# Seven PSUM banks as slices of one tensor, and reductions and exponentials of two banks at once

## The chip, the cores and the metric

The kernel runs on one core of a Trainium2 chip. The core has TensorE (PE in the profile, its weight loads PEld), VectorE (DVE), ScalarE (ACT), GpSimd (POOL) and SyncE (SP), which issues the transfers. TensorE writes its results to PSUM, eight banks of 512 fp32 columns on 128 partitions. The metric is the device time of one execution in microseconds, lower is better.

## The reference

One transformer block on x of 2048 tokens by 512, all in fp32: a layer norm with scale and shift from a condition c, attention with 32 heads of 16, and a spatial-shift MLP.

```python
qkv = (x @ wqkv).reshape(B, S, 3, H, Dh).transpose(2, 0, 3, 1, 4)
q, k, v = qkv[0], qkv[1], qkv[2]
scores = jnp.einsum("bhqd,bhkd->bhqk", q, k) * (Dh ** -0.5)
p = _softmax(scores, axis=-1)
o = jnp.einsum("bhqk,bhkd->bhqd", p, v)
...
x = x + ga * _A_ref(h, A_wqkv, A_wo)
h = _layernorm(x, axis=-1) * (1 + cb) + sb
x = x + gb * _B_ref(h, B_w1, B_w2, B_w3, B_w4)
```

The change touches the scores and the softmax, and none of the rest.

## The kernel before, in words

The kernel has three stages. The first normalizes x and makes q, k and v of the first heads. The second, the attention, goes over 64 units (4 chunks of 512 queries by 16 pairs of heads), with 16 steps of 128 keys in each unit, 1,024 steps in all. The rest of the projections is mixed into it, and the beginning of the MLP into its end. The third stage is the MLP.

A step s has two halves, one for each head of the pair (j = 0, 1). A half step makes one score tile (`sc`: 128 keys by 512 queries, `score_part`) and, `LEAD` = 24 steps ahead, one maxima tile (`mb`: 128 queries by 512 keys, `max_part`). The matmuls of these two use different halves of TensorE's rows, so they are written next to each other (`row_pair`). DVE takes the maximum of each row of `mb` into `mx` (L992); after 32 such tiles `max_fin` turns the maxima of a unit into two extra rows of q, by 8 small transfers. ACT takes the exponential of `sc` into P (`pt`, L1008). P is stored as 32-bit integers whose upper 16 bits are read as one fp16 part, the lower as another; `p_low` makes the lower part on POOL (L1061) or, where POOL is behind, on ACT (L156). `pv_part` then multiplies both parts by v, four matmuls of 32 columns side by side (L1083, L1086), into one more bank, `pv`.

The order of the instructions is written out by a planner, the class `Sched`, while the program is built: it has a clock for each engine and costs for each instruction, and the main loop goes over blocks of `GRP` = 3 half steps. In a block come the matmuls of three score and three maxima tiles, their evictions, and then three `pv` parts of a block two earlier. What is left of PE's time is filled with projection work by `sch.fill`. The class `Slots` holds when each of the `NSM` = 7 shared banks comes free, by the planner's clock. Before, each bank is a tensor of its own, made anew for each tile under one of seven tags, and takes the slot that is free first. Projection tiles and the small `ot` tile (`o_fin`, a transposition of the sum) take their banks from the same seven (`dbank`).

The semaphores that each instruction waits for do not stand in the code. They are put in when the program is built, from the tensors that the instructions read and write.

```python
    def bank(nm):
        x = sm.take()
        return x, ap_.tile([P, CH], F32, name=nm, tag=f"s{x}", bufs=1)
```

Of the kernel before, what the change touches and what calls it, by code (L numbers as in the profile page):

```python
# [20 lines left out]
S, D, H, DH, F = 2048, 512, 32, 16, 1792  # L21
P = 128
KT = D // P
NKT = S // P
CH = 512
NC = S // CH
# [11 lines left out]
LEAD = 24  # L38
# [3 lines left out]
PX = 270.0  # L42
XX = 170.0
XP = {"A": 280.0, "D": 200.0, "G": 200.0}
# [4 lines left out]
CROW, CCOL, CIN, CMID, COUT = 232.0, 240.0, 105.0, 95.0, 67.0  # L49
CFILL = 200.0  # L50
NSM = 7
# [3 lines left out]
LATE = 1e9  # L55
# [41 lines left out]
XCOPY = 0  # L97
NQ = 7
NPT = 6
NV = 3  # L100
DBW, DLAT = 360.0, 2200.0
NST = 4
# [9 lines left out]
class Sched:  # L112
# [29 lines left out]
    def chain(self, *ops, prio=1, ready=None, bank=None):  # L142

        if ready is None:
            ready = self.T["P"] + PX
        n = 0
        while n < len(self.chains) and self.chains[n][2] <= prio:
            n += 1
        bank = bank is not None and id(bank.tensor)
# [100 lines left out]
    def share(self, slots, most):  # L250

        self.avail, self.back, self.owner = [], [], {}
        self.slots, self.most = slots, most

    def take(self, tile):
# [7 lines left out]
        self.owner[id(b.tensor)] = i  # L263
        self.open = id(b.tensor)
        return b

    def free(self, b):

        i = self.owner.pop(id(b.tensor), None)
# [35 lines left out]
class Slots:  # L305
# [7 lines left out]

    def late(self):
        return sum(t == LATE for t in self.t)


def cA(n=CH):
# [12 lines left out]
def kernel(ctx, tc, A_x, A_wqkv, A_wo, B_w1, B_w2, B_w3, B_w4, c, w_mod, out):  # L331
    nc = tc.nc
    te, act, dve, pool, dma = nc.tensor, nc.scalar, nc.vector, nc.gpsimd, nc.sync
# [56 lines left out]
    for j in range(2):  # L390
        x = [ident[:, 64 * j + VD * a:64 * j + VD * a + DH + 1] for a in range(3)]
# [116 lines left out]
    kst, qtl = [], []  # L508
# [226 lines left out]
    for i in range(NV):  # L735
        t = qp.tile([P, H // 4, 192], BF16, name=f"vt{i}")
# [218 lines left out]

    unit_tiles(at, 1, pool, pool)
    qst, vst, mxs = {}, {}, {}
    pv, pt = {}, {}

    def load_unit(u):  # L960
        ci, pr = units[u]
# [11 lines left out]
    sm = Slots(NSM)  # L973
    e_exp, e_hi, e_low, v_free, acs = {}, {}, {}, [0.0], []

    def bank(nm):
        x = sm.take()
        return x, ap_.tile([P, CH], F32, name=nm, tag=f"s{x}", bufs=1)

    def max_part(m, j):  # L980

        u, i = divmod(m, 16)
        c, g = divmod(i, 4)
        if u not in mxs:
            mxs[u] = at.tile([P, 2, 4, NC], F32, name="mx", tag="mx", bufs=2)
        x, b = bank("mb")
        ready, sm.t[x] = sm.t[x], LATE
        r = slice(64 * j, 64 * j + 62)
        lhs = qst[u][r, (g // 2) * 256:(g // 2 + 1) * 256].rearrange("p (n l) -> p l n", l=2)[:, g % 2]

        def after(e):
            end = sch.crit("D", 605, e + PX, lambda: dve.reduce_max(mxs[u][:, j, g, c:c + 1], b, axis=AX.X))  # L992
            sm.t[x] = end + XP["D"]
            if (c, g, j) == (NC - 1, 3, 0):
                max_fin(u)
        return ready, lambda: te.matmul(b, lhs, kst[u % 3][r, c * CH:(c + 1) * CH], start=True, stop=True), after  # L996

    def score_part(s, j):

        u, kt = divmod(s, NKT)  # L1000
        if j == 0:
            pt[s] = at.tile([P, 2, CH], I32, name="pt", tag="pt", bufs=NPT)
        x, b = bank("sc")
        ready, sm.t[x] = sm.t[x], LATE
        r = slice(64 * j, 64 * j + 64)

        def after(e):
            ea = sch.crit("A", 480, e + PX, lambda: act.activation(pt[s][:, j], b, AF.Exp))  # L1008
            sm.t[x] = ea + XP["A"]
            if j:  # L1010
                e_exp[s] = e_hi[s] = ea
        return ready, lambda: te.matmul(b, kst[u % 3][r, kt * P:(kt + 1) * P], qst[u][r], start=True, stop=True), after  # L1012

    def row_pair(s, j):

        parts = []
        if 0 <= s < NS:
            parts.append((j, score_part(s, j)))
        if s + LEAD < NS:
            parts.append((1 - j, max_part(s + LEAD, 1 - j)))  # L1020
        parts = [x for _, x in sorted(parts, key=lambda x: x[0])]

        def mms():
            for _, mm, _ in parts:
                mm()
        e = sch.put("P", CROW, max(x[0] for x in parts), mms)
        return [partial(x[2], e) for x in parts]

    def max_fin(u):
        mf = at.tile([P, 8], F32, name="mf", tag="mf", bufs=2)  # L1030
        nm = at.tile([P, 2, 8], F32R, name="nm", tag="nm", bufs=2)
        mx = mxs.pop(u)

        def shift_rows():
            for j in range(2):
                for i in range(2):
                    r = 64 * j + 62 + i
                    for h in range(2):
                        sch.dma(dma.dma_start,
                                qst[u][r:r + 1, h * 256:(h + 1) * 256].bitcast(F32).rearrange("o (p l) -> o p l", l=2),  # L1040
                                nm[:, i, 4 * j + 2 * h:4 * j + 2 * h + 2].bitcast(F32))
        sch.chain(("D", 85, lambda: dve.reduce_max(mf.rearrange("p (j g) -> p j g", j=2), mx, axis=AX.X)),
                  ("A", 100, lambda: act.activation(mf, mf, AF.Copy, scale=-1.0, bias=PEXP)),
                  ("A", 100, lambda: act.activation(nm[:, 0], mf, AF.Copy)),
                  ("G", 250, lambda: pool.tensor_tensor(nm[:, 1], mf, nm[:, 0], op=OP.subtract)),
                  (None, 0, shift_rows), mark(("shift", u)), prio=0, ready=sch.T["D"])

    def p_low(s):

        p = pt[s].rearrange("p j n -> p (j n)")  # L1050
        o, i = p.bitcast(F16)[:, 0::2], p.bitcast(U16)[:, 0::2]
        ready = e_exp.pop(s) + XX
        g, a = [max(sch.T[e], ready) for e in "GA"]
        if g > a + LACT:

            for h in range(NLOW):
                n = 2 * CH // NLOW
                c = slice(h * n, (h + 1) * n)
                e_low[s] = XP["A"] + sch.crit("A", CLOW, ready, partial(act.activation, o[:, c], i[:, c], AF.Copy, scale=0.5))
        else:  # L1060
            e_low[s] = XP["G"] + sch.crit("G", 1345, ready, lambda: pool.tensor_scalar(  # L1061
                o, i, 0.5, 1.0, op0=OP.mult, op1=OP.mult))
# [5 lines left out]
    def pv_part(s, lo):  # L1068


        u, kt = divmod(s, NKT)
        if kt == 0 and not lo:
            pv[u] = ap_.tile([P, CH], F32, name="pv", tag="v", bufs=1)
        v, acc = vst[u], pv[u]

        def mms():
            for j in range(2):
                for i in range(2):
                    r = 64 * j + 32 * i
                    if lo:  # L1080
                        c = 128 + 32 * j + (0 if i else 8)
                        n = min(32, 192 - c)
                        te.matmul(acc[r:r + n, :], v[:, kt + i, c:c + n].bitcast(F16), pt[s + i].bitcast(F16)[:, j, 0::2],  # L1083
                                  start=False, stop=kt == NKT - 2, skip_group_check=True)
                    else:
                        te.matmul(acc[r:r + 32, :], v[:, kt, r:r + 32], pt[s].bitcast(F16)[:, j, 1::2],  # L1086
                                  start=kt == 0, stop=False, skip_group_check=True)
        e = sch.put("P", CCOL, 0.0, mms)
        if lo:
            for i in range(2):  # L1090
                pt.pop(s + i)
                e_low.pop(s + i)
            if kt == NKT - 2:
                acs.append((u, e + COUT))
# [507 lines left out]
    for k, blk in enumerate(blocks + [[]] * (LAG + CPER)):  # L1602
# [21 lines left out]
        banks = sorted(sm.t)  # L1624
        n = 0
        for s, i in row:
            n += (s >= 0) + (s + LEAD < NS)

            start = max(start, banks[n - 1 + 2 * (s < 0)] - t)
            t += CROW  # L1630
        t += CMID
        for s, i in col:
            start = max(start, pv_ready(s, i) - t)
# [2 lines left out]
        sch.flush(need)  # L1636
        sch.T["P"] = max(sch.T["P"], start) + CIN
        low = sorted(e_exp)
        for s, i in row:
# [91 lines left out]
```

## Time and profile before

| | |
|---|---|
| median of 3 runs | 2018.74 us (2018.37 to 2018.93) |
| profiled execution, span from first to last instruction | 2019.7 us |
| stage 1, up to the first maxima matmul | 96.6 us |
| attention, up to the last `pv` matmul | 1436.7 us |
| stage 3 | 486.4 us |
| mean granted TensorE clock | 0.992 of full speed |

The profiled execution is shown by its span, 0.05% over the median; the two are taken as one. In the page's rows an instruction is named by engine, line, operation and the tiles that it writes and reads (`mx<-mb`), with its count, the busy time in us and the mean of one in ns. A row of waits names the engine that waited and who ended the wait. PEclk is the clock that TensorE was granted, as a share of full speed.

### The profile page before, as it was taken

Reading aid. Unit: us, or ns where it says so; the run is one execution under the profiler, and the core shown is the slowest. Engines: PE = TensorE matmul, PEld = TensorE weight load, DVE = VectorE, ACT = ScalarE, POOL = GpSimd, SP = SyncE. Lnnn points to the kernel's source line nnn. Section 1 sums busy time; section 2 is a strip of 40 time slices with the busy share of each in tenths; the row PEclk is TensorE's granted clock in tenths of the full one; section 3 lists DMA queues with packets and bytes.
Section 4 is the critical chain, followed back from the end, with each engine's and each line's share of the span. In section 5 each row is a group of like instructions: output and inputs, shape, how many; then the busy total and the mean of one; then the engine's idle time right before and its main releaser. Section 6 shows DMA issues by size and latency. Waiting matters only on the chain.

```text
span 2019.7 us, 41655 instructions
## 1 busy us (share of the span) xinstructions
PE 1934.4 (96%) x14456; PEld 1162.1 (58%) x14456; DVE 1656.3 (82%) x2979; ACT 1510.2 (75%) x3085; POOL 1571.9 (78%) x1488
## 2 busy tenths in 40 slices
PE   7999999999999999999999999999998999999999
PEld 5755545454444444444444444444455878898998
DVE  6398888879999999999999999999975886556443
ACT  6438987768999999999999999999985544344443
POOL 6349988879999999999999999999996554435222
PEclk9989999999999999999999999999999999999999
DMA  8777675445343434444443435354414676553541
GB/s 295 233 204 192 151 187 155 135 130 124 86 92 87 91 88 83 96 82 97 81 98 75 104 72 107 72 136 126 99 46 158 230 261 265 226 200 116 201 153 68
DMA packets 185508, 278.01 MB, mean 138 GB/s; under 512 B 117104, under 2 KB 127856, under 8 KB 169008
## 3 DMA queue, kind: packets, MB, share of 16 engines
q1 hardware_dynamic: 181792, 267.20, 49.1%
q10 hardware_dynamic: 2304, 4.20, 0.6%
q0 software_dynamic: 1200, 3.93, 0.5%
q8 instruction: 115, 1.88, 0.4%
q14 instruction: 97, 0.79, 0.1%
HBM read 211.81 MB, written 62.91 MB: 136 GB/s over the span
## 4 chain that ended last, share of the span: by engine, by line
PE 61%; DVE 16%; ACT 9%; issue 6%; POOL 4%; DMA 3%; SPq 0%; ACTq 0%; POOLq 0%; DVEq 0%
PE mb L996 13%; DVE mx L992 12%; PE pv L1086 9%; PE sc L1012 8%; ACT pt L1008 7%; PE w L363 5%; PE w L359 5%; PE w L361 5%; PE pv L1083 4%; PE ot L1113 3%; POOL pt L1061 2%; PE xT L1247 1%; POOL trs L1356 1%; PE v L359 1%; DMA wr<-Ws 1%
## 5 line engine op out<-in xcount | busy, mean ns | idle before, releaser
L1061 POOL TENSOR_SCALAR pt<-pt 128x1024 f16<-128x1024 uint16 x953 | 1248.3, 1367 | 79.9 <-ACT pt L1008 76.7
L992 DVE TENSOR_REDUCE mx<-mb 128x1 f32<-128x512 f32 x2048 | 1250.0, 681 | 72.7 <-PE mb L996 63.5
L1008 ACT ACTIVATE pt<-sc 128x512 int32<-128x512 f32 x2048 | 1060.9, 614 | 123.5 <-PE mb L996 97.1
L996 PE MATMUL mb<-kst,qtl 62*128 62x512 f32 x2048 | 781.1, 461 | 20.5 <-ACT pt L1008 10.0
L1012 PE MATMUL sc<-qtl,kst 64*128 64x512 f32 x2048 | 739.3, 449 | 4.6 <-DVE mx L992 1.8
L996 PEld LDWEIGHTS mb<-kst,qtl 62*128 62x128 f32 x2048 | 358.9, 193 | 233.7 <-ACT pt L1008 160.4
L1012 PEld LDWEIGHTS sc<-qtl,kst 64*128 64x128 f32 x2048 | 336.6, 185 | 185.4 <-DVE mx L992 118.7
L1086 PE MATMUL pv<-pt,vst 128*32 128x512 f16 x4096 | 384.8, 397 | 20.6 <-ACT ac L1103 20.6
L1460 POOL TENSOR_TENSOR g<-sq,g 128x256 fp32r<-128x256 f32 (+1 forms) x124 | 96.8, 785 | 188.9 <-ACT g L1459 176.6
L1083 PE MATMUL pv<-pt,vst 128*32 128x512 f16 (+1 forms) x2048 | 220.8, 389 | 2.5 <-POOL pt L1061 2.4
L1086 PEld LDWEIGHTS <-vst 128*32 128x32 bf16 x4096 | 91.8, 93 | 227.2 <-issue 208.8
L361 PE MATMUL w<-A,wr 128*128 128x256 f32 (+1 forms) x520 | 153.4, 295 | 0.3 <-DVE A L349 0.3
L359 PE MATMUL w<-A,wr 128*128 128x256 f32 (+1 forms) x520 | 153.2, 295 | 0.3 <-ACT A L353 0.3
L363 PE MATMUL w<-A,wr 128*128 128x256 f32 (+1 forms) x520 | 153.1, 294 | 0.0
L1456 ACT ACTIVATE sq<-w 128x256 f32<-128x256 f32 (+1 forms) x130 | 52.1, 401 | 127.0 <-PE w L363 117.5
L363 PE MATMUL w<-wr,g 128*128 128x512 f32 x270 | 106.5, 394 | 3.1 <-POOL g L1460 3.1
L359 PE MATMUL w<-wr,g 128*128 128x512 f32 x270 | 106.9, 396 | 1.8 <-DMA wr<-Ws 1.8
L361 PE MATMUL w<-wr,g 128*128 128x512 f32 x270 | 106.1, 393 | 0.0
L1438 DVE SCALAR_TENSOR_TENSOR sq<-sq,w 128x256 f32<-128x256 f32 (+1 forms) x130 | 58.1, 449 | 56.5 <-ACT sq L1458 56.3
L359 PEld LDWEIGHTS w<-A,wr 128*128 128x128 f32 x520 | 98.7, 190 | 1.7 <-ACT A L353 0.5
L361 PEld LDWEIGHTS w<-A,wr 128*128 128x128 f32 x520 | 98.7, 190 | 1.6 <-DVE A L349 0.5
L363 PEld LDWEIGHTS w<-A,wr 128*128 128x128 f32 x520 | 98.6, 190 | 0.5 <-issue 0.5
(156 smaller groups left out, 2131.6 us busy)
## 6 DMA issues: line engine op xcount, KB each, us to landing
wr<-Ws SPq DMA_DIRECT2D x66, 1024.0 KB, 5.2
vst<-Vs SPq DMA_DIRECT2D x64, 768.0 KB, 5.7
kst<-Ks SPq DMA_DIRECT2D x126, 384.0 KB, 6.1
Ws<-wr SPq DMA_DIRECT2D x14, 1024.0 KB, 5.0
qtl<-Qs SPq DMA_DIRECT2D x128, 96.0 KB, 4.3
Vs<-vt SPq DMA_DIRECT2D x32, 384.0 KB, 4.2
Ks<-qk SPq DMA_DIRECT2D x16, 512.0 KB, 3.8
Qs<-qk SPq DMA_DIRECT2D x16, 512.0 KB, 3.0
```

Source lines behind the costliest of these rows:

```text
L359: te.matmul(o, lh, rh, start=first, stop=False)
L361: te.matmul(o, lh, rl, start=False, stop=False)
L363: te.matmul(o, ll, rh, start=False, stop=last)
L992: end = sch.crit("D", 605, e + PX, lambda: dve.reduce_max(mxs[u][:, j, g, c:c + 1], b, axis=AX.X))
L996: return ready, lambda: te.matmul(b, lhs, kst[u % 3][r, c * CH:(c + 1) * CH], start=True, stop=True), after
L1008: ea = sch.crit("A", 480, e + PX, lambda: act.activation(pt[s][:, j], b, AF.Exp))
L1012: return ready, lambda: te.matmul(b, kst[u % 3][r, kt * P:(kt + 1) * P], qst[u][r], start=True, stop=True), after
L1061: e_low[s] = XP["G"] + sch.crit("G", 1345, ready, lambda: pool.tensor_scalar(o, i, 0.5, 1.0, op0=OP.mult, op1=OP.mult))
L1083: te.matmul(acc[r:r + n, :], v[:, kt + i, c:c + n].bitcast(F16), pt[s + i].bitcast(F16)[:, j, 0::2], start=False, stop=kt == NKT - 2, skip ...
L1086: te.matmul(acc[r:r + 32, :], v[:, kt, r:r + 32], pt[s].bitcast(F16)[:, j, 1::2], start=kt == 0, stop=False, skip_group_check=True)
L1113: te.matmul(b[:, t * n:(t + 1) * n], ac[:, t * P:(t + 1) * P], smat.rearrange("p j d -> p (j d)"), start=True, stop=True)
L1460: ("G", cG(n), lambda: pool.tensor_tensor(lo, sq, hi, op=OP.subtract)), (None, 0, end), bank=b)
```

## The change

The seven banks become the slices `psb[:, i]` of one tensor, and the six buffers of P the slices of one tensor `pts`. Where two tiles of one kind lie in neighbouring banks, DVE reduces both with one instruction of 1,024 columns (`max_out`), and ACT takes the exponential of both with one (`score_out`). In a block of three half steps the first tile of each kind stays single and the other two are joined. `choose` asks `Slots.place` for banks for these groups, and falls back to single tiles if the joined ones would start over 150 ns later by the planner's clock. The maxima `mx` are stored in the order in which the tiles come, and `max_fin` reads them in the permuted order.

```diff
+    psb = ap_.tile([P, NSM, CH], F32, name="psb")
+    pts = at.tile([P, NPT, 2, CH], I32, name="pts")
...
-        return sch.take(lambda i: psd["d"].tile([P, CH], F32, name=n, tag=f"s{i}" if psd["s"] else f"d{i}", bufs=1))
+        return sch.take(lambda i: psb[:, i] if psd["s"] else psd["d"].tile([P, CH], F32, name=n, tag=f"d{i}", bufs=1))
...
-        def after(e):
-            end = sch.crit("D", 605, e + PX, lambda: dve.reduce_max(mxs[u][:, j, g, c:c + 1], b, axis=AX.X))
-            sm.t[x] = end + XP["D"]
+    def max_out(x, ts, e):
+        n = len(ts)
+        u, i = divmod(ts[0][0], 16)
+        o = 2 * i + 1 - ts[0][1]
+        b = psb[:, x:x + n]
+        end = sch.crit("D", 72 + 533 * n, e + PX, lambda: dve.reduce_max(mxs[u][:, o:o + n], b, axis=AX.X))
+        sm.t[x:x + n] = [end + XP["D"]] * n
...
-        def after(e):
-            ea = sch.crit("A", 480, e + PX, lambda: act.activation(pt[s][:, j], b, AF.Exp))
-            sm.t[x] = ea + XP["A"]
+    def score_out(x, ts, e):
+        n = len(ts)
+        s, j = ts[0]
+        o = 2 * (s % NPT) + j
+        p = pts.rearrange("p a j n -> p (a j) n")[:, o:o + n]
+        ea = sch.crit("A", 53 + 427 * n, e + PX, lambda: act.activation(p, psb[:, x:x + n], AF.Exp))
+        sm.t[x:x + n] = [ea + XP["A"]] * n
...
+                n = 2 if two and on and (len(tiles) - i) % 2 == 0 and not cut(tiles[i + 1][1]) else 1
+                out.append((tiles[i:i + n], fn, fin))
...
-        sch.chain(("D", 85, lambda: dve.reduce_max(mf.rearrange("p (j g) -> p j g", j=2), mx, axis=AX.X)),
+        sch.chain(("D", 85, lambda: dve.reduce_max(mf.rearrange("p (j g) -> p j g", j=2),
+                                                   mx.rearrange("p (c g j) -> p j g c", g=4, j=2), axis=AX.X)),
...
-        for s, i in row:
-            for fn in row_pair(s, i):
-                fn()
+        if row:
+            row_pairs(row, *choose(row)[1:])
```

In the built program DVE's 2,048 reductions become 738 single and 655 joined ones, ACT's 2,048 exponentials 696 single and 676 joined; POOL makes 1,020 lower parts of P in the attention stage in place of 952. The matmuls and transfers keep their number. The order of instructions shows what each one waits for, in square brackets: the semaphore of an engine (`PE_49`, `Activation_49` for ACT, `DVE_49`, `Pool_49` for POOL), which counts the instructions that this engine has finished.

DVE before, in the middle of the attention, at the end of a unit (`rc` belongs to the `ot` tile of a unit, `mf` closes the maxima of another):

```order
L992 TENSOR_REDUCE mx<-mb 128x1 [waits PE_49] x30
L1128 RECIPROCAL rc<-sm 128x8 [waits Activation_49,Pool_49]
L992 TENSOR_REDUCE mx<-mb 128x1 [waits PE_49] x2
L992 TENSOR_REDUCE mx<-mb 128x1 [waits DVE_49,PE_49]
L1042 TENSOR_REDUCE mf<-mx 128x8 [waits DVE_49,Pool_49]
```

DVE now, at the end of a unit in the middle of the attention:

```order
L1032 TENSOR_REDUCE mx<-psb 128x1 [waits PE_49]
L1194 RECIPROCAL rc<-sm 128x8 [waits Activation_49,Pool_49]
L1032 TENSOR_REDUCE mx<-psb 128x2 [waits PE_49,Activation_49]
L1108 TENSOR_REDUCE mf<-mx 128x8 [waits DVE_49]
L1032 TENSOR_REDUCE mx<-psb 128x1 [waits Activation_49]
L1032 TENSOR_REDUCE mx<-psb 128x2 [waits Activation_49]
```

Before, a reduction waits for PE's matmul; now most of them, single (128x1) or joined (128x2), wait for ACT as well or for ACT alone.

ACT before, behind the small instructions that close the maxima of a unit:

```order
L1043 ACTIVATE mf<-mf 128x8 [waits DVE_49]
L1044 ACTIVATE nm<-mf 128x8 [waits DMAHW4_49,DMAHW3_49,DMAHW5_49,DMAHW2_49,DMAHW6_49,DMAHW1_49,DMAHW7_49,DMAHW0_49,Activation_49]
L1008 ACTIVATE pt<-sc 128x512 [waits PE_49]
L1008 ACTIVATE pt<-sc 128x512 [waits PE_49,Pool_49]
L1008 ACTIVATE pt<-sc 128x512 [waits PE_49]
```

ACT now, at the same place:

```order
L1110 ACTIVATE mf<-mf 128x8 [waits DVE_49]
L1111 ACTIVATE nm<-mf 128x8 [waits DMAHW4_49,DMAHW3_49,DMAHW5_49,DMAHW2_49,DMAHW6_49,DMAHW1_49,DMAHW7_49,DMAHW0_49,Activation_49]
L1043 ACTIVATE pts<-psb 128x512 [waits PE_49,Pool_49]
L1043 ACTIVATE pts<-psb 128x1024 [waits DVE_49,PE_49,Pool_49]
L1043 ACTIVATE pts<-psb 128x512 [waits DVE_49]
L1043 ACTIVATE pts<-psb 128x1024 [waits DVE_49,Pool_49]
```

Three of these four exponentials wait for a DVE reduction; before, none did.

PE now, the matmuls of one block in the middle of the attention, between two runs of `pv`:

```order
L1150 MATMUL pv<-pts,vst 32x512
L1024 MATMUL psb<-qtl_145,kst_147 128x512 [waits Activation_49]
L1018 MATMUL psb<-kst_967,qtl_965 128x512
L1018 MATMUL psb<-kst_967,qtl_965 128x512 [waits DVE_49]
L1024 MATMUL psb<-qtl_145,kst_147 128x512 x2
L1018 MATMUL psb<-kst_967,qtl_965 128x512
```

and before, of one block there:

```order
L1086 MATMUL pv<-pt,vst 32x512
L1012 MATMUL sc<-qtl_1103,kst_1105 128x512 [waits DVE_49]
L996 MATMUL mb<-kst_967,qtl_965 128x512 [waits Activation_49] x2
L1012 MATMUL sc<-qtl_1103,kst_1105 128x512 [waits DVE_49] x2
L996 MATMUL mb<-kst_967,qtl_965 128x512 [waits Activation_49]
```

Before, each matmul waits for the engine that read its own bank last; now the block has two waits, one ahead of the first half step and one ahead of the other two, on the reader that ran last.

More of the change, by code (lines that the diff above doesn't have):

```diff
@@ L99 @@
 NPT = 6
+DMX, DSC = 1, 1
+DTOL = 150.0
 NV = 3
@@ L148, in chain @@
             n += 1
-        bank = bank is not None and id(bank.tensor)
+        bank = bank is not None and self.key(bank)
         if bank == self.open:
@@ L974, with max_tile @@
     e_exp, e_hi, e_low, v_free, acs = {}, {}, {}, [0.0], []
[L976 to L980, printed above, removed]
+    def max_tile(m, j, b):
         u, i = divmod(m, 16)
@@ L996, in max_part, with score_tile @@
[L996 to L998 removed]
+        te.matmul(b, lhs, kst[u % 3][r, c * CH:(c + 1) * CH], start=True, stop=True)
+    def score_tile(s, j, b):
         u, kt = divmod(s, NKT)
[L1001 to L1004, printed above, removed]
         r = slice(64 * j, 64 * j + 64)
[L1007 to L1009 removed]
+        te.matmul(b, kst[u % 3][r, kt * P:(kt + 1) * P], qst[u][r], start=True, stop=True)
```

112 lines of the change are left out of this document (79 added, 33 removed).

## The prediction

> **What bounds the kernel now.** I read the page's first two lines, then the windows by stage, the groups by line, the chain of waits, and last the order of instructions of both programs with what each waits for.
>
> ```profile
> span 2019.7 us, 41655 instructions
> PE 1934.4 (96%) x14456; PEld 1162.1 (58%) x14456; DVE 1656.3 (82%) x2979; ACT 1510.2 (75%) x3085; POOL 1571.9 (78%) x1488
> ```
>
> The windows cut the span at the first maxima matmul and behind the last `pv` matmul. The columns are the window, its length, busy time and count of each engine, the granted TensorE clock, the DMA share and GB/s:
>
> ```profile
> 0.00:96.60 96.60, 83.53 (x420) 62.77 (x420) 47.06 (x109) 54.21 (x106) 45.72 (x66) 0.98 0.82 265
> 96.60:1533.30 1436.70, 1390.13 (x11313) 687.08 (x11314) 1312.05 (x2273) 1243.27 (x2489) 1324.01 (x1135) 0.99 0.48 111
> 1533.30:2019.70 486.40, 460.79 (x2724) 412.29 (x2722) 297.18 (x597) 212.75 (x492) 202.18 (x287) 0.99 0.52 191
> ```
>
> The attention stage is the middle row, 1436.7 us, and there four engines are each 87 to 97% busy side by side. The change touches only this stage; the 96.6 + 486.4 = 583 us around it stay. The work of the stage by groups (mean ns of one behind the bar, then idle time ahead of it and its releaser):
>
> ```profile
> L992 DVE TENSOR_REDUCE mx<-mb 128x1 f32<-128x512 f32 x2048 | 1250.0, 681 | 72.7 <-PE mb L996 63.5 <-PE sc L1012 5.4
> L1061 POOL TENSOR_SCALAR pt<-pt 128x1024 f16<-128x1024 uint16 x953 | 1248.3, 1367 | 79.9 <-ACT pt L1008 76.7
> L1008 ACT ACTIVATE pt<-sc 128x512 int32<-128x512 f32 x2048 | 1060.9, 614 | 123.5 <-PE mb L996 97.1 <-PE sc L1012 15.3 <-POOL pt L1061 1.2
> ```
>
> DVE and ACT wait for PE (63.5 and 97.1 us in all), hardly for anything else. PE's weight loads wait for a bank that one of them read last:
>
> ```profile
> PEld mb L996 <- ACT pt L1008: 160.4, 464, 0.9
> PEld sc L1012 <- DVE mx L992: 118.7, 303, 2.2
> ```
>
> 2048 score tiles in blocks of three are 683 blocks, so a block takes about 1436.7/683 = 2.1 us, and 1.8 us where no projection work is mixed in: the timeline shows 17 reductions in 10.25 us, 0.603 us each back to back, and three of them are 1.81 us.
>
> ```profile
> 902.21 10.25 DVE L992 TENSOR_REDUCE mx<-mb 128x1 f32<-128x512 f32 x17 [0.42 <-PE mb L996]
> 902.24 3.05 ACT L1008 ACTIVATE pt<-sc 128x512 int32<-128x512 f32 x6 [0.41 <-PE mb L996]
> ```
>
> These two rows also show what matters most here: DVE and ACT read PSUM at the same time, one bank each, for the whole stage, while PE fills others.
>
> **The change, part by part.** Two joined instructions replace two pairs of single ones per block: that saves DVE and ACT each one fixed cost. Against this stands what the order above shows: once all seven banks are one tensor, every DVE reduction that follows an exponential waits for it, every exponential that follows a reduction waits for that, and PE's matmuls wait for whichever came last. Followed through the built program by the counts that its waits name, every one of the 7,897 reads and writes of `psb` stands behind all earlier ones of the other engines, whatever the bank; of the reads and writes of single banks before, almost none did. So the stage becomes one chain, and its time is the sum of the links, not the largest engine.
>
> A block now is: matmuls of the first half step; exponential of 512 and reduction of 512 (in either order, one behind the other); matmuls of the other two half steps; exponential of 1,024 and reduction of 1,024, one behind the other. Two half steps need two pairs of matmuls. The links at full clock and at half clock (the granted clock was 0.50 in 136.25 to 143.07, the windows below):
>
> ```profile
> 901.65 0.49 PE L1012 MATMUL sc<-qtl,kst 64*128 64x512 f32 x1
> 901.65 0.72 PE L996 MATMUL mb<-kst,qtl 62*128 62x512 f32 x2
> 136.57 0.79 PE L1012 MATMUL sc<-qtl,kst 64*128 64x512 f32 x1 [1.84 <-DVE mx L992]
> 137.40 0.60 ACT L1008 ACTIVATE pt<-sc 128x512 int32<-128x512 f32 x1 [1.98 <-PE mb L996]
> 137.77 1.22 PE L1012 MATMUL sc<-qtl,kst 64*128 64x512 f32 x2
> ```
>
> One half step takes 0.50 us at full clock and 0.79 at half, two take 0.74 and 1.22; ACT starts 0.04 after the matmul's end (136.57 + 0.79 = 137.36, 137.40), and alone it takes 0.60. From ACT's end to DVE's start it is 0.03 (1545.05 to 1545.08):
>
> ```profile
> 1544.63 0.42 ACT L1458 ACTIVATE sq<-sq 128x256 f32<-128x256 f32 x1 [0.56 <-DVE sq L1457]
> 1545.08 0.42 DVE L1438 SCALAR_TENSOR_TENSOR sq<-sq,w 128x256 f32<-128x256 f32 x1 [0.48 <-ACT sq L1458]
> ```
>
> From ACT's or DVE's end to the matmul I take 0.05. No instruction of 1,024 PSUM columns runs before; the slopes of two widths give it:
>
> ```profile
> L1457 DVE SCALAR_TENSOR_TENSOR sq<-sq,w 128x256 f32<-128x256 f32 x102 | 42.7, 419 | 32.0 <-ACT sq L1456 27.6
> L1457 DVE SCALAR_TENSOR_TENSOR sq<-sq,w 128x384 f32<-128x384 f32 x28 | 15.3, 551 | 10.7 <-ACT sq L1456 10.7
> L1456 ACT ACTIVATE sq<-w 128x256 f32<-128x256 f32 x102 | 38.6, 378 | 119.8 <-PE w L363 113.2 <-DMA x<-in_A_x_dram 2.6 <-POOL g L1460 0.8
> L1456 ACT ACTIVATE sq<-w 128x384 f32<-128x384 f32 x28 | 13.5, 486 | 7.2 <-PE w L363 4.3 <-POOL g L1460 2.8
> ```
>
> DVE 1.03 ns per column, so 0.68 + 512 x 1.03 = 1.21 us; ACT 0.84, so 0.60 + 0.43 = 1.03. The upper ends are twice the single one, 1.36 and 1.20 (+0.32 per block, +215 us); a lower end under the slope has nothing for it.
>
> Per block at half clock: 0.84 + 0.04 + 0.60 + 0.03 + 0.68, then 1.27 + 0.04 + 1.03 + 0.03 + 1.21 = 5.77 us. At full clock 0.55 and 0.79 stand for 0.84 and 1.27: 5.00 us. 667 blocks have both kinds of tile; the first 16 have maxima alone and the last 16 scores alone (4.08 and 3.81 us at half clock). Half clock: 667 x 5.77 + 16 x 7.89 = 3975 us. Full clock: 667 x 5.00 + 16 x 6.36 = 3437 us.
>
> Other work in `psb` joins the chain: 312 matmuls of 512 and 215 of 256 columns (0.23 and 0.12 us at full clock), 64 times `ot` with its copy, and the evictions of the projections:
>
> ```profile
> 1819.21 0.23 PE w L359
> 1799.96 0.12 PE w L359
> 914.67 1.08 PE L1113 MATMUL ot<-smat,ac 128*128 128x34 f32 x8
> L1120 ACT ACTIVATE sm<-ot 128x136 f32<-128x136 f32 x63 | 18.0, 286 | 20.5 <-PE ot L1113 20.4
> L353 ACT ACTIVATE qk<-q 128x512 fp32r<-128x512 f32 x14 | 8.5, 609 | 2.9 <-PE q L363 2.8
> ```
>
> 72 + 26 + 69 us of PE, and about 85 of ACT and DVE (18 for `sm`, 28 splits at 0.61 with as many subtractions, and 17 `v` tiles): 250 us, at half clock some 380.
>
> What I cost at nothing: `pv`, 12 matmuls a block in three groups of four. At full clock they take 0.86 us (900.86 to 901.72), at half clock some 1.5, by the third row:
>
> ```profile
> 900.86 0.41 PE L1086 MATMUL pv<-pt,vst 128*32 128x512 f16 x4
> 901.32 0.40 PE L1086 MATMUL pv<-pt,vst 128*32 128x512 f16 x4
> 140.28 0.62 PE L1086 MATMUL pv<-pt,vst 128*32 128x512 f16 x4
> ```
>
> They run under the long exponential and reduction (2.3 us). The 1,020 low halves of P, now nearly all on POOL, take 1.37 us each, 1.5 per block, 2.1 of 5.8 us; the ring of P has six slots as before, so its waits reach as far back. The permuted `mf` reduction runs 64 times at some 0.2 us. If `pv` came late, the next block's matmuls would stand behind it on PE.
>
> **The clock.** PE is now idle for most of a block, and the trace shows what short idleness does. Windows of 3.41 us, in pairs or threes that follow each other:
>
> ```profile
> 102.12:105.53 3.41, 2.42 (x6) 0.94 (x6) 3.41 (x7) 1.61 (x5) 0.00 (x0) 1.00 1.11 260
> 105.53:108.94 3.41, 3.41 (x10) 2.28 (x9) 3.41 (x7) 0.29 (x1) 2.94 (x3) 0.50 0.99 157
> 132.83:136.25 3.42, 1.91 (x7) 0.90 (x7) 3.35 (x5) 1.54 (x3) 1.67 (x2) 1.00 1.06 346
> 136.25:139.66 3.41, 2.69 (x10) 1.74 (x10) 3.41 (x7) 1.63 (x4) 2.74 (x3) 0.50 1.09 221
> 139.66:143.07 3.41, 3.41 (x22) 1.42 (x23) 3.41 (x7) 2.93 (x7) 3.41 (x3) 0.50 0.99 203
> 480.99:484.40 3.41, 2.25 (x24) 1.13 (x26) 3.41 (x7) 3.41 (x7) 2.85 (x3) 1.00 1.00 194
> 484.40:487.82 3.42, 3.42 (x34) 2.17 (x27) 2.22 (x4) 2.92 (x7) 3.15 (x3) 1.00 0.48 173
> ```
>
> After 1.91 and after 2.42 us busy of 3.41 (with six or seven matmuls) the clock was 0.50; after 2.25 (24 matmuls) it stayed. At 0.50, 2.69 us busy did not bring it back; fully busy windows came ahead of its return. The changed block at full clock has 0.50 + 0.74 + 0.86 (`pv`) = 2.1 us busy of 5.0, or 1.4 per 3.41: under every one of these, so the clock falls. At half clock it is 0.79 + 1.22 + 1.5 = 3.5 of 5.77, or 2.1 per 3.41, under the 2.69 that did not suffice: it stays down. Only the bursts of projection work in the first fifth of the stage should lift it now and then; I take 85 us off for them. The Trainium skill, "TensorE: Matmul & The Clock Gate", Part 1, has the clock halve after at least one idle window of about 3.4 us and return after a busy one. Taken literally, as no idle time over 3.4 us, it would leave this kernel at full clock, since no link pair here is that long; the row at 132.83, with 1.91 us busy, does not agree with that reading.
>
> Sum at half clock: 583 + 3975 + 380 - 85 = 4853, and some 15 us for copies of `ac` and the like: **4870 us**. Its span and the runs agree (2019.7 against a median of 2018.7), so nothing is added.
>
> **The rivals.** (1) The chain is as told, but the clock stays up, because the gate counts idle stretches and not shares: 583 + 3437 + 250 + 15 = 4285 us. For it: the longest idle stretch of PE in a block is under 2.4 us. Against: the row at 132.83.
> (2) The two readers run beside each other and only PE takes turns with them; then a block is the longer of each two, 0.84 + 0.04 + 0.68 + 1.27 + 0.04 + 1.21 = 4.08 us, and the time 683 x 4.08 + 300 + 583 = 3670 us. It decides if a reader's wait names an access at least a phase back; the order has it at the one just before.
> (3) Faster: the waits are met before they are reached, and the change does what it says. DVE would spend 0.60 + 1.14 = 1.74 instead of 1.81 us per block, at best 0.07 x 683 = 48 us less, 1971 us; POOL, at 1324 of 1437 us, would let some 30 through: 1985 us. It decides if ACT's exponential always ends before DVE's turn comes, which needs idle time that engines over 87% busy do not have. The Trainium skill, "PSUM — Partial Sum Buffer", Specifications, says that ScalarE and VectorE can read PSUM in parallel at full rate if they do not meet in one bank; the rows at 902.21 and 902.24 agree. By that the order between banks is not needed, but the program waits for it all the same.
>
> **How the numbers follow.** The chain at half clock for most of the stage 0.66, at full clock 0.21, (2) 0.09, (3) 0.03, no visible change 0.01 (0.2% is about what the measurement can tell). The range reaches from just under (1) to the likeliest with most of the upper ends of the joined instructions, 4870 + 215: 4200 to 5100 us.
>
> **What would show it.** In the profile after: the waits led by DVE for ACT and ACT for DVE on `psb`; PEclk at 5 or 6 tenths through the stage; reductions of 1,024 at 1.21 and exponentials at 1.03 us; a stage of some 4.3 ms and an unchanged last 486 us; no engine over 50% busy but PE. Clock digits of 9 mean rival (1). Reductions and exponentials that overlap in the timeline mean (2) or (3), and my reading of the waits was wrong.

## The result and the profile after

| | before | after |
|---|---|---|
| median of the runs | 2018.84 us (2018.37 to 2026.94) | 5093.45 us (5092.2 to 5095.95, 4 runs) |
| span of the profiled execution | 2019.7 us | 5091.2 us |
| mean granted TensorE clock | 0.992 | 0.567 |

The ratio is 2.5216, 95% interval 2.5166 to 2.5265: the changed kernel takes two and a half times as long. The page of after, its span, the busy time of each engine, and the clock in 40 slices:

```profile
span 5091.2 us, 40365 instructions
...
PE 3009.8 (59%) x14456; PEld 1435.8 (28%) x14456; DVE 1734.2 (34%) x2324; ACT 1491.7 (29%) x2341; POOL 1688.7 (33%) x1556
...
PEclk8555555555555555555555555555555555559999
```

The work is what it was, DVE 1734 us against 1656 and ACT 1492 against 1510, but no engine is the bound any more: DVE is busy for a third of the span, where it was for 82%. The windows by stage (length, busy time and count of PE, PEld, DVE, ACT and POOL, then clock, DMA share and GB/s) show where the time went:

```profile
0.00:96.60 96.60, 84.02 (x423) 63.04 (x423) 47.76 (x110) 54.54 (x107) 47.16 (x67) 0.98 0.83 269
96.60:4600.00 4503.40, 2463.27 (x11329) 959.01 (x11329) 1391.90 (x1624) 1226.76 (x1749) 1441.13 (x1207) 0.51 0.14 35
4600.00:5091.00 491.00, 462.55 (x2706) 413.74 (x2706) 294.56 (x590) 210.45 (x486) 200.46 (x284) 0.98 0.52 189
```

All of it is in the attention, 1437 us before and 4503 now; the stages around it are as they were. The groups of the two readers by shape (count, busy us, mean ns of one, then idle time ahead and who ended it):

```profile
L1032 DVE TENSOR_REDUCE mx<-psb 128x2 f32<-128x1024 f32 x655 | 802.3, 1225 | 1401.7 <-ACT pts L1043 757.1 <-PE psb L1024 608.8 <-PE psb L1018 35.7
L1043 ACT ACTIVATE pts<-psb 128x1024 int32<-128x1024 f32 x676 | 691.9, 1023 | 1626.1 <-DVE mx L1032 883.2 <-PE psb L1018 702.9 <-PE psb L1024 39.0
L1032 DVE TENSOR_REDUCE mx<-psb 128x1 f32<-128x512 f32 x738 | 510.4, 692 | 1388.6 <-ACT pts L1043 902.2 <-PE psb L1024 443.7 <-PE psb L1018 42.8
L1043 ACT ACTIVATE pts<-psb 128x512 int32<-128x512 f32 x696 | 415.2, 597 | 1190.6 <-DVE mx L1032 854.2 <-PE psb L1018 306.0 <-PE psb L1024 27.3
```

A joined instruction is cheap beside two single ones that run alone, 1,225 ns against 2 x 692 and 1,023 against 2 x 597. Beside the kernel before it saves nothing in all: there the single ones followed each other so closely that the 2,048 reductions took 1,250 us together and the exponentials 1,061 (their rows stand in the prediction), and here, single and joined together, they take 1,313 and 1,107 us. And DVE stands idle 2,790 us ahead of its reductions and ACT 2,817 us ahead of its exponentials, each for more than half of that time until the other has ended. The same in the view of waits (us in total, times, longest):

```profile
ACT pts L1043 <- DVE mx L1032: 1737.5, 618, 6.6
DVE mx L1032 <- ACT pts L1043: 1659.3, 667, 6.4
PEld psb L1024 <- ACT pts L1043: 1288.1, 646, 3.8
PEld psb L1018 <- DVE mx L1032: 1271.3, 605, 2.6
DVE mx L1032 <- PE psb L1024: 1052.5, 667, 4.6
ACT pts L1043 <- PE psb L1018: 1008.9, 643, 16.2
```

Before, what DVE and ACT waited for on a bank was PE. One block in the timeline (start, duration; in brackets the idle time before and its releaser):

```profile
2502.93 0.79 PE L1024 MATMUL psb<-qtl,kst 64*128 64x512 f32 x1 [1.53 <-ACT pts L1043]
...
2503.83 0.60 ACT L1043 ACTIVATE pts<-psb 128x512 int32<-128x512 f32 x1 [0.46 <-PE psb L1018]
2504.46 0.69 DVE L1032 TENSOR_REDUCE mx<-psb 128x1 f32<-128x512 f32 x1 [2.69 <-ACT pts L1043]
2505.20 0.79 PE L1018 MATMUL psb<-kst,qtl 62*128 62x512 f32 x1 [1.48 <-DVE mx L1032]
2505.21 1.22 PE L1024 MATMUL psb<-qtl,kst 64*128 64x512 f32 x2
...
2506.52 1.02 ACT L1043 ACTIVATE pts<-psb 128x1024 int32<-128x1024 f32 x1 [2.09 <-PE psb L1018]
...
2507.57 1.23 DVE L1032 TENSOR_REDUCE mx<-psb 128x2 f32<-128x1024 f32 x1 [2.43 <-ACT pts L1043]
...
2508.85 0.79 PE L1018 MATMUL psb<-kst,qtl 62*128 62x512 f32 x1 [1.03 <-DVE mx L1032]
...
2510.48 0.60 ACT L1043 ACTIVATE pts<-psb 128x512 int32<-128x512 f32 x1 [2.94 <-DVE mx L1032]
```

Left out are the weight loads, the second matmul of each pair, `pv` and POOL, which run beside these. Each row starts where the one above has ended: matmul, exponential, reduction, matmuls, exponential, reduction, and at 2508.85 the next block, 5.92 us later. Before, a block took about 2.1 us.

### The profile page after: what moved, and what is told of

It is laid out like the page before. It is cut to its first block, busy times and chain, and to the rows that moved or that the text cites. A ratio compares the mean times of both kernels' runs of the same rounds, so it can differ in the third digit from the quotient of the medians.

```text
span 5091.2 us, 40365 instructions
## 1 busy us (share of the span) xinstructions
PE 3009.8 (59%) x14456; PEld 1435.8 (28%) x14456; DVE 1734.2 (34%) x2324; ACT 1491.7 (29%) x2341; POOL 1688.7 (33%) x1556
## 4 chain that ended last, share of the span: by engine, by line
PE 42%; DVE 27%; ACT 23%; issue 4%; DMA 2%; POOL 1%; ACTq 0%; SPq 0%; DVEq 0%; POOLq 0%
DVE mx L1032 26%; ACT pts L1043 21%; PE psb L1024 14%; PE psb L1018 14%; PE psb L1179 2%; PE w L392 2%; PE w L388 2%; PE w L390 2%; PE psb L388 1%; PE psb L390 1%; PE psb L392 1%; DMA kst<-Ks 1%; ACTq L1043 0%; ACT sm L1186 0%; DMA raw<-in_B_w_dram 0%
## 5 line engine op out<-in xcount | busy, mean ns | idle before, releaser
L1032 DVE TENSOR_REDUCE mx<-psb 128x1 f32<-128x512 f32 (+1 forms) x1393 | 1312.7, 942 | 2790.3 <-ACT pts L1043 1659.3
L1128 POOL TENSOR_SCALAR pts<-pts 128x1024 f16<-128x1024 uint16 x1021 | 1359.1, 1332 | 2677.2 <-ACT pts L1043 2638.2
L1043 ACT ACTIVATE pts<-psb 128x1024 int32<-128x1024 f32 (+1 forms) x1372 | 1107.1, 807 | 2816.8 <-DVE mx L1032 1737.5
L1018 PE MATMUL psb<-kst,qtl 62*128 62x512 f32 x2048 | 1365.7, 733 | 937.1 <-DVE mx L1032 912.0
L1024 PE MATMUL psb<-qtl,kst 64*128 64x512 f32 x2048 | 1358.7, 731 | 886.7 <-ACT pts L1043 841.4
L1024 PEld LDWEIGHTS psb<-qtl,kst 64*128 64x128 f32 x2048 | 525.7, 294 | 1356.3 <-ACT pts L1043 1288.1
L1018 PEld LDWEIGHTS psb<-kst,qtl 62*128 62x128 f32 x2048 | 530.8, 296 | 1332.6 <-DVE mx L1032 1271.3
L1153 PE MATMUL pv<-pts,vst 128*32 128x512 f16 x4096 | 595.2, 610 | 0.0
L1150 PE MATMUL pv<-pts,vst 128*32 128x512 f16 (+1 forms) x2048 | 325.2, 623 | 1.1 <-POOL pts L1128 1.1
L1179 PE MATMUL psb<-smat,ac 128*128 128x34 f32 x512 | 121.0, 404 | 90.9 <-DVE mx L1032 74.1
```

The lines of the kernel that those rows point to most:

```text
L1032: end = sch.crit("D", 72 + 533 * n, e + PX, lambda: dve.reduce_max(mxs[u][:, o:o + n], b, axis=AX.X))
L1043: ea = sch.crit("A", 53 + 427 * n, e + PX, lambda: act.activation(p, psb[:, x:x + n], AF.Exp))
L1153: te.matmul(acc[r:r + 32, :], v[:, kt, r:r + 32], pt(s).bitcast(F16)[:, j, 1::2], start=kt == 0, stop=False, skip_group_check=True)
L1179: te.matmul(b[:, t * n:(t + 1) * n], ac[:, t * P:(t + 1) * P], smat.rearrange("p j d -> p (j d)"), start=True, stop=True)
```

## The experiments

The theory (A) is that of the prediction: one tensor puts every access of the seven banks in one order, and the idle TensorE then gets half the clock. The main rival (B) is that the joined instructions themselves, the new choice of banks or the ring of P are to blame. Nine kernels were run.

### One tensor, nothing joined

```diff
-DMX, DSC = 1, 1
+DMX, DSC = 0, 0
```

> The changed kernel with joining switched off: seven banks as slices of one tensor, every reduction and exponential single (512 columns). Theory A (one tensor puts all accesses of the banks in one line): per half step 0.84 (matmul at half clock, with its release) + 0.05 + 0.60 + 0.05 + 0.69 + 0.05 = 2.28 us, 6.85 per block of three, against 5.9 joined; 667 x 6.85 + 150 for the first and last blocks + the 420 us of other work that the changed kernel's stage has, + 590 outside = about 5,700 us (5,500 to 5,900), granted clock near 0.5 in the stage, no reduction overlapping an exponential. Rival B (the joined instructions hold two banks too long, one tensor is harmless): about 2,020 us, as before.

Measured: 5655.03 us (one run), clock 0.56. Its waits and a piece of its timeline:

```profile
ACT pts L1043 <- DVE mx L1032: 2188.8, 946, 6.0
DVE mx L1032 <- ACT pts L1043: 2185.2, 986, 5.6
```

```profile
3001.82 0.79 PE L1018 MATMUL psb<-kst,qtl 62*128 62x512 f32 x1 [1.48 <-DVE mx L1032]
...
3002.66 0.69 DVE L1032 TENSOR_REDUCE mx<-psb 128x1 f32<-128x512 f32 x1 [0.89 <-PE psb L1024]
3003.39 0.60 ACT L1043 ACTIVATE pts<-psb 128x512 int32<-128x512 f32 x1 [2.34 <-DVE mx L1032]
...
3004.04 0.79 PE L1024 MATMUL psb<-qtl,kst 64*128 64x512 f32 x1 [1.42 <-ACT pts L1043]
```

This is inside the 5,500 to 5,900 us of theory A. The loss is there without a single joined instruction, and larger. Inside the one chain, joining gains 562 us (5655 to 5093), since it takes links out of it. So it is not the joined instructions that lose the time; the one tensor, the ring of P and the choice of banks are left.

### Seven tensors, nothing joined

```diff
-    psb = ap_.tile([P, NSM, CH], F32, name="psb")
+    BANKS = [1] * 7
+    pst = [ap_.tile([P, w, CH], F32, name=f"psb{i}") for i, w in enumerate(BANKS)]
...
-DMX, DSC = 1, 1
+DMX, DSC = 0, 0
```

Everywhere, `psb[:, x]` becomes the tensor in which bank x lies. The ring of P, the new order of `mx` and `choose` stay.

> The kernel of the first experiment (one tensor, joining off) with one edit: the seven banks are seven tensors. The ring of P and the new way to choose banks stay. Theory A (one tensor puts all accesses in one line, and nothing else in the change costs): back to the kernel before, 2,019 us within 1%, granted clock 0.99. Rival D (the ring of P or the choice of banks costs too): 2,040 us or more.

Measured: 2042.58 us (2041.31 to 2043.71), ratio 1.0107, interval 1.0087 to 1.0126. The number of tensors alone is worth 5655 - 2043 = 3612 us. So the loss is that of the one tensor. The 22 us that are left lie just above A's 1% and reach D's limit of 2,040: the ring of P or the choice of banks costs a little too, and the last two experiments look at that.

### Two tensors, one for each reader

`BANKS` is [3, 3, 1]: maxima only in the first three banks, scores only in the next three, projections and `ot` in the last; joined as in the change.

> Joined instructions as in the change, but the banks in three tensors: three banks for maxima, three for scores, one for projection and ot tiles. DVE and ACT then never read one tensor, and only PE takes turns with each of them. This tells what the order between the two readers costs apart from PE's. Theory A: a block is 0.55 + 0.05 + 0.69 + 0.79 + 0.05 + 1.23 = 3.4 us at full clock, 4.1 at half, since the exponentials run beside the reductions; PE is busy 2.1 of 3.4 us, 62%, so the clock stays up for the most part: 683 x 3.4 + 250 to 350 + 590 = about 3,200 us (3,000 to 3,700). Rival B (only the joining costs): about 5,000 us, as the change. Rival C (only the order between DVE and ACT costs, PE's turns are hidden): about 2,050 us.

Measured: 3611.52 us (one run), clock 0.642. The readers now start together:

```profile
2000.14 0.69 DVE L1043 TENSOR_REDUCE mx<-psb 128x1 f32<-128x512 f32 x1 [1.00 <-PE psb L1029]
2000.17 0.60 ACT L1054 ACTIVATE pts<-psb 128x512 int32<-128x512 f32 x1 [1.10 <-PE psb L1029]
...
2002.18 1.22 DVE L1043 TENSOR_REDUCE mx<-psb 128x2 f32<-128x1024 f32 x1 [1.34 <-PE psb L1029]
...
2002.20 1.02 ACT L1054 ACTIVATE pts<-psb 128x1024 int32<-128x1024 f32 x1 [1.44 <-PE psb L1029]
```

Taking apart the two readers, and both from the projections, thus gives back some 1,480 us of the loss (5093 to 3612), the change of the clock included. Some 1,570 us are left (3612 to 2043): the turns that PE still takes with each reader and the low clock, and with them whatever the joins and the fixed shares of banks cost, which this run doesn't separate. The time is above the 3,200 us that I expected, within the range given: the clock, which I had thought to stay up for the most part, was 0.52 in the middle of the stage (2000 to 3000 us), although PE was busy for 757 of these 1,000 us.

### Three times as many `pv` matmuls

Each of the 12 `pv` matmuls of a block is issued three times into the same sum. This gives TensorE more to do in the time in which it waits; the sums of P times v and of P become three times as large, and their quotient stays.

```diff
-            for j in range(2):
+            for rep, j in ((rep, j) for rep in range(3) for j in range(2)):
```

> The changed kernel with each pv matmul issued three times into the same accumulation, so the weighted values and their sums are both tripled and the quotient stays. It adds 24 matmuls per block to PE where it is idle under the long exponential and reduction (2.4 us). Theory A (the clock was halved because PE was idle too much): the added work makes PE busy over two thirds of the time, the granted clock returns to over 0.9 in most of the stage, the matmuls of a block take 0.50 and 0.74 instead of 0.79 and 1.22 us, a block about 5.2 instead of 5.9 us, and the whole about 4,450 us (4,350 to 4,700): faster than the change with more work. Rival B (the clock is low for another reason, so the added matmuls run at half clock, 4.3 us per block in place of 1.5): 1.9 us more per block, about 6,400 us.

Measured: 4985.37 us (one run). With 12,288 matmuls more it is 108 us faster than the change. The page and the timeline:

```profile
PE 3466.9 (70%) x26744; PEld 1643.9 (33%) x26744; DVE 1732.7 (35%) x2324; ACT 1495.7 (30%) x2341; POOL 1696.8 (34%) x1556
...
PEclk8577777777777777777777777777777777789999
```

```profile
2999.40 1.03 ACT L1043 ACTIVATE pts<-psb 128x1024 int32<-128x1024 f32 x1 [2.73 <-DVE mx L1032]
...
3000.24 0.85 PE L1150 MATMUL pv<-pts,vst 128*32 128x512 f16 x12
...
3001.02 0.18 PEld L1024 LDWEIGHTS psb<-qtl,kst 64*128 64x128 f32 x1 [0.45 <-issue]
3001.02 0.50 PE L1024 MATMUL psb<-qtl,kst 64*128 64x512 f32 x1
...
3006.18 0.50 PE L1018 MATMUL psb<-kst,qtl 62*128 62x512 f32 x1 [1.64 <-DVE mx L1032]
...
3008.16 0.79 PE L1024 MATMUL psb<-qtl,kst 64*128 64x512 f32 x1 [1.47 <-ACT pts L1043]
```

More work on TensorE does raise its clock, so it is idleness that lowers it: from 5 tenths to 7 in the slices, by turns of full clock (a half step in 0.50 us) and half clock (0.79). A block at full clock takes 5.16 us here (3001.02 to 3006.18) against 5.92. The expected 4,450 us was missed for two reasons that the rows show: the clock came up only in part, and the tripled `pv` was no longer hidden. At 3000.43 the last reader had ended, yet the matmuls start at 3001.02, behind `pv`. So the run settles that the work on TensorE sets the clock, and does not measure the clock's share of the loss; from the two blocks an estimate of that is 667 x 0.76 = some 500 us of 3,074.

### Pairs of banks as tensors, tiles anywhere

`BANKS` is [2, 2, 2, 1], with joins inside a pair; single tiles take any bank.

> Joined instructions as in the change, with the seven banks as three tensors of two banks and one of one bank, so that a joined pair has a tensor of its own and order arises only inside a pair. Theory A (the joining itself is cheap, one tensor was the whole loss): near the kernel before, 2,000 to 2,080 us, with reductions of 1,024 columns at 1.22 us and DVE under its former load. Rival B (joining costs by itself, two neighbouring banks being held until both tiles are there and both are read): over 2,200 us.

Measured: 2368.59 us (2360.05 to 2374.54), ratio 1.1735, interval 1.1713 to 1.1757. Far from A's 2,000 to 2,080, and on B's side of 2,200. I had taken pairs to be small enough to be nearly free of the order. They are not, where two tiles of different kinds share one:

```profile
DVE mx L1042 <- PE psb L1028: 240.0, 463, 3.0
PEld psb L1028 <- ACT pts L1053: 198.5, 274, 1.7
```

The weight load of a maxima tile (L1028) waits for the exponential of a score tile in 274 places, 198.5 us; in the kernel with seven tensors these were 20 places and 6.2 us. (The kernel before has 160.4 us of such waits too, for single banks that ACT had read last.) DVE's wait for the matmul is 240 us, where it was 75.4 with seven tensors and 63.5 before. Followed through the built program, 765 of the 7,997 reads and writes of the banks wait for an access to another bank of their tensor that comes after the last one to their own; 545 of these are matmuls. Whether the rest of the loss is order too, or the time that two banks are held, this run doesn't tell.

### Pairs for joined tiles, single banks for single ones

`BANKS` is [2, 2, 1, 1, 1], and a penalty in `place` keeps joined tiles in the pairs and single tiles in the other three banks; projections and `ot` take these three as well. In the built program 181 of the 8,014 reads and writes of the banks still wait for an access to another bank of their tensor.

> Joined instructions, banks as two tensors of two banks and three of one; joined pairs take the tensors of two, single tiles those of one (a tensor of two only where nothing else is left), so that DVE and ACT hardly ever meet in one tensor. This tells what part of the loss with pair tensors (2,368 us) was order between the two tiles of unlike kind that shared a pair. Theory A (the rest of the loss is bank time): a pair of banks is held for 0.05 + 0.74 + 0.04 + 1.22 + 0.05 = 2.1 us, and each of the two pair tensors is needed once per block, so a block takes 2.1 us or a little more instead of 1.83: 2,019 + 683 x 0.27 = about 2,200 us (2,150 to 2,300). Rival B (the joined instructions themselves are slow): 2,350 us or more. Rival E (all of the loss was order inside the pairs): 2,000 to 2,030 us.

Measured: 2203.94 us (2197.2 to 2207.78), ratio 1.0902, interval 1.0876 to 1.0928. B's limit of 2,350 is not reached, and A's number is met: keeping the kinds apart gives back 165 us of the 326 that the pairs had cost over seven single tensors, without a change to the joined instructions (1,220 and 1,027 ns). What is left is as expected from how long banks are held: two banks are blocked from the first of two matmuls to the end of one long reader, and PE's matmuls wait. Nor do the joins relieve the readers. The page has 1271.7 us for all reductions and 1080.9 us for all exponentials, where the kernel with seven tensors has 1252.6 and 1070.1:

```profile
L1046 DVE TENSOR_REDUCE mx<-psb 128x1 f32<-128x512 f32 (+1 forms) x1445 | 1271.7, 908 | 217.2 <-PE psb L1032 162.4
L1057 ACT ACTIVATE pts<-psb 128x512 int32<-128x512 f32 (+1 forms) x1425 | 1080.9, 785 | 339.5 <-PE psb L1038 157.5
```

The windows of 500 to 1400 us, of the kernel with seven tensors and of this one:

```profile
500.00:1400.00 900.00, 857.55 (x7282) 405.14 (x7280) 850.64 (x1474) 822.11 (x1618) 847.52 (x722) 0.99 0.43 93
```

```profile
500.00:1400.00 900.00, 835.66 (x6720) 369.74 (x6712) 796.32 (x963) 708.97 (x1028) 844.71 (x715) 0.99 0.39 84
```

PE does 8% fewer matmuls in these 900 us and is 22 us less busy. DVE is 6% less busy, no more than that slower pace accounts for; of ACT's 14%, a part is the lower halves of P that POOL has taken over (6 on ACT in the whole run, against 71). That the banks' time is what holds it back is the reading that forecast this number; the banks were not varied by themselves.

### Only exponentials joined

`BANKS` is [2, 1, 1, 1, 1, 1], `DMX, DSC = 0, 1`: one pair for joined exponentials, all maxima single.

> Only the exponentials are joined; one tensor of two banks for the joined pair, five of one bank for all single tiles. Theory A (bank time decides): the pair is held 0.05 + 0.74 + 0.04 + 1.02 + 0.05 = 1.9 us per block against 1.83 of a block before, and DVE runs as before, so 2,050 us (2,010 to 2,120). Rival F (a fixed cost less per block on ACT pays): under 2,010 us.

Measured: 2062.9 us (2061.34 to 2065.59), ratio 1.0204, interval 1.0185 to 1.0223. As expected, and 20 us above the same kernel with nothing joined. The exponentials take 1,056 us in all against 1,070, and the program is slower all the same.

### The last 22 us: ring of P or choice of banks

Two kernels start from the one with seven tensors. The first makes P anew for each step, as before:

```diff
-    pts = at.tile([P, NPT, 2, CH], I32, name="pts")
...
+            ptd[s] = at.tile([P, 2, CH], I32, name="pt", tag="pt", bufs=NPT)
```

> Seven tensors and single tiles (the version that took 2,043 us), but P again as a new tile for each step, six buffers, in place of slices of one tensor. Theory R: the 22 us that the version with seven tensors keeps over the kernel before come from the ring of P, whose slices order POOL's lower parts, ACT's exponentials and the pv matmuls more than single tiles do; then this takes 2,018 to 2,026 us. Theory K: they come from the choice of banks; then it stays at 2,038 to 2,048 us. In between means both.

The second keeps the ring and gives the tiles of a block the banks in the order in which these come free, as before:

```diff
+            n = sorted(range(len(gs)), key=lambda g: (gs[g][0][0][0], gs[g][0][0][1][1]))
+            xs = [x for _, x in sorted(zip(n, sorted(range(NSM), key=lambda i: sm.t[i])))]
```

> Seven tensors, single tiles and the ring of P (the version that took 2,043 us), but the tiles of a block take the banks in the order in which these come free, as before the change, in place of the first arrangement that starts as early by the planner's clock. Theory K (choice of banks): 2,018 to 2,028 us, since a block's first matmul no longer waits for a bank that was read late. Theory R (ring of P): it stays at 2,038 to 2,048 us.

Measured: 2044.54 us (ratio 1.0117, interval 1.0093 to 1.0141) without the ring, 2028.8 us (1.0039, 1.0027 to 1.005) with the banks in order. The ring of P costs nothing that can be measured. The choice of banks is some 14 of the 22 us, 0.8 us over K's range and far from R's: `place` takes the first arrangement that starts as early by the planner's clock, so that a bank that comes free late can go to a first matmul; that this is how the time is lost was only argued. The remaining 8 us were not traced further.

No variant beats the kernel before.

## Why the prediction was right, and where it was off

The forecast was 4,870 us, the result 5,093, inside 4,200 to 5,100 by 7 us. The mechanism was right, and that the range held is in part luck: its upper end allowed 215 us for joined instructions as long as two single ones, which did not come, and the 223 us that were missing lay in terms for which the range had no room.

**The chain: shown.** The waits led by DVE for ACT and ACT for DVE, the reductions and exponentials that never overlap (before, one of each ran at the same time for 1,001 us in all, now for none), and the last stage of 491 us are as announced. That this comes from the one tensor is shown by the kernels with one and with seven tensors and nothing joined.

**The clock: shown.** PEclk is 5 in nearly all slices of the attention, which rules out rival (1), and the kernel with three times the `pv` shows that idleness causes it. The literal reading of the Trainium skill, "TensorE: Matmul & The Clock Gate", Part 1, under which this kernel would stay at full clock for want of an idle window of 3.4 us, is refuted here: in the attention of the changed kernel the longest stretch between two matmuls without one running was 3.10 us, and the clock fell to half 26 times; it was 0.51 over 4,503 us, with PE busy for 2,463 of them.

**Rivals (2) and (3): refuted.** Readers beside each other would have given 3,670 us; the kernel built to have that, with two tensors, took 3,612 (its projections stand apart as well, so the two numbers are not the same sum). For (3) the waits would have had to be met early; they are 1,737 and 1,659 us.

**The joined instructions: right.** 1,225 ns and 1,023 ns against 1.21 and 1.03 us from the slopes of other rows; the upper ends, twice a single one, are refuted. That the joins would relieve DVE by little was right as well: rival (3) had 1.14 us for one that follows another without a gap, and in the kernel with pairs kept apart such reductions start 1.14 us apart, where single ones before start 0.60 apart, so that two cost 1.20.

**The handovers: too small.** I took 0.04 us from PE to ACT and 0.03 from reader to reader. In the block above ACT starts 0.11 and 0.09 us after the matmuls' end, and in the next one ACT starts 0.10 us after DVE (2509.69 + 0.69 to 2510.48). From ACT to DVE it is the 0.03 that I took (2503.83 + 0.60 to 2504.46). The row of that reduction:

```profile
2509.69 0.69 DVE L1032 TENSOR_REDUCE mx<-psb 128x1 f32<-128x512 f32 x1 [0.89 <-PE psb L1024]
```

The block is 5.92 us and not 5.77, which is 667 x 0.15 = 100 us of the 223 that are missing; 0.12 of the 0.15 are the two handovers from PE to ACT, and the rest is mostly the reductions, 0.69 and 1.23 us for 0.68 and 1.21.

**Other work less the 85 us of relief: too little.** The score matmuls alone (L1024: busy time and count of PE and PEld, then clock, DMA share and GB/s) in two windows of 1,000 us, one with projections and one without:

```profile
250.00:1250.00 1000.00, 262.36 (x400) 101.74 (x400) 0.53 0.19 52
2000.00:3000.00 1000.00, 326.50 (x486) 126.46 (x486) 0.50 0.12 27
```

486 tiles are 162 blocks of 6.17 us each, 0.25 over the bare block for `ot` and the like, or 171 us in all. 400 tiles are 133 blocks, so that the projections took 1000 - 133 x 6.17 = 179 us of the first window alone. The attention's 4,503 us less 667 x 5.92 and the ends (16 x 7.89) leave some 428 us of other work, where the sum had 380 + 15 - 85 = 310. The 85 us are the likeliest error: the clock in the window with projections is 0.53, so that bursts of projection work, each cut into links of the same chain, hardly raise it. No run separates the three terms of that sum, though, and their shares of the 118 us stay open. The 100 and the 118 us, and 5 us in the last stage, make up the 223.

**What went wrong in the expectations.** Pairs of banks were held to be harmless, and cost 17%; with two tensors the clock was expected to stay up, and was 0.52; its rise under three times the `pv` was taken as whole, and the `pv` as hidden.

## What to carry to other kernels

Before tiles of several engines become slices of one tensor, count who then waits for whom in the built program: the engines here were ordered by the tensor and not by the bank, and the tensor that an instruction needed to save 0.16 us, or 0.06 in a row of its kind, turned a pipeline of four engines into one chain. If joined reads are wanted, the tensor may span only what one reader reads at once, and the price is then, as far as these runs go, that two banks are held until the long read ends. An engine that falls idle in such a chain can lose its clock as well, so a chain is to be costed at the low clock.

## What the runs showed of the hardware that was not expected

The clock can halve without a long idle stretch. In the attention of the changed kernel no stretch without a matmul was longer than 3.10 us, and the clock fell 26 times; with two tensors none was longer than 1.58 us, and it fell 61 times. In the changed kernel it then stayed at 0.50 from 1160 to 4519 us, with PE shown busy for 534 us in 1,000 and, in these 1,000 us, no wait of a maxima matmul for DVE longer than 1.9 us (third row). The rows are the maxima matmuls of the change from 1100 to 4500 us, all its instructions in 1,000 us of that, and the wait of its maxima matmuls for DVE there:

```profile
1100.00:4500.00 3400.00, 1105.83 (x1641) 430.22 (x1641) 0.50 0.12 29
...
2000.00:3000.00 1000.00, 534.23 (x2548) 191.86 (x2548) 317.09 (x360) 277.14 (x384) 331.31 (x273) 0.50 0.12 27
...
PE psb L1018 <- DVE mx L1032: 230.5, 151, 1.9
```

The same 1,000 us of the kernel with three times the `pv`, and of the kernel with two tensors:

```profile
2000.00:3000.00 1000.00, 667.42 (x5559) 253.93 (x5563) 322.18 (x365) 282.53 (x390) 338.65 (x277) 0.75 0.13 28
```

```profile
2000.00:3000.00 1000.00, 756.55 (x3688) 280.42 (x3686) 456.17 (x519) 405.27 (x556) 478.40 (x395) 0.52 0.20 44
```

The share of busy time alone does not decide: the clock was 0.75 with 667 us busy, and 0.52 with 757. In the traces of all eleven kernels the clock changes in steps of 3.41 us, and where it came back to full speed, PE had been busy for 2.79 us or more of the step just before (2.91 or more in the changed kernel). That did not always suffice: with two tensors 113 steps with 2.9 us or more were followed by another at half. What holds the clock up has no sharp boundary here: in the attention with three times the `pv` it held after a step with 1.68 us busy and fell after one with 2.37.

One reduction of 1,024 columns over two banks costs 1,225 ns and one exponential 1,023 ns, 159 and 171 ns less than two single ones, where each instruction runs alone on its tensor. Where they follow each other without a gap, the saving shrinks: starts of joined ones lie 1.14 and 0.92 us apart (pairs kept apart, medians), those of single ones 0.60 and 0.48 (before). A handover to ACT takes longer than one to DVE: in the changed kernel from 1160 to 4500 us the medians are 0.10 us from PE to ACT and 0.09 from DVE to ACT, and 0.05 from PE to DVE and 0.03 from ACT to DVE.
